# Swapping two matmuls at each seam between the w_out products and the w_in products of a second MLP layer

## Chip, core and metric

One NeuronCore of a Trainium2 chip runs the whole program. The metric is the device time in microseconds (us) from launch to end; lower is better.

## What is computed

The program is an attention (local heads and strided heads) followed by two MLP layers. Only the second layer matters here:

```
def _moe2_ref(x, w_in, w_out):
    h = np.maximum(x @ w_in, 0.0)
    return (h * h @ w_out).astype(np.float32)      # x: 2304 x 512, w_in: 512 x 2048, w_out: 2048 x 512
```

## The kernel before

Every fp32 operand is split into a high part and a remainder, so that one exact product is made of three TensorE matmuls: high by high, high by remainder, remainder by high.

Layer 2 walks over blocks of 512 tokens. After a first narrow block, four blocks `k` remain, and for each of them the 2048 columns of w_in are taken 256 at a time, `q` = 0 to 7. A step (k, q) is called a pair; there are 32 (`pairs7`). Both products of a pair are computed by a scheme with seven half-sized multiplications instead of eight. In a pair, TensorE alternates between two kinds of work, all of it in matmuls of 128 x 128 stationary by 256 moving columns:

- a **visit** (`visit`, line 1279 in the traces of this kernel) multiplies by w_in and accumulates in one PSUM bank, `ps_m`. There are four visits to a pair, of 12, 6, 12 and 12 matmuls. All four use the same bank: pool `ps_h` has a single buffer. The first matmul of each visit starts the bank afresh.
- a **gap** (`gaps`, filled by `n_unit`, line 1306) multiplies the squared activations of the pair before by w_out and accumulates in seven other banks (`ps_y`). There are four gaps, after visits 1, 2, 3 and 4, of 9, 9, 15 and 9 matmuls. I number a gap by the visit that it follows; gap 4 stands ahead of visit 1 of the next frame.

`frame` is called 31 times in `seven`, and writes one pair's order down by hand: TensorE executes the 84 matmuls of a frame in the order of the text (visit 1, gap 1, visit 2, gap 2, visit 3, gap 3, visit 4, gap 4). Between two visits, VectorE or ScalarE reads the bank of the visit that has just ended, and only after that may the next visit start it again:

- visit 1: ScalarE copies the bank out (line 1359), 128 x 512
- visit 2: VectorE adds half the bank to `c11` (helper `add`, line 1112), 128 x 256
- visit 3: VectorE reads it twice (line 1112): 128 x 512 into `u`, then 128 x 256 into `a22`
- visit 4: VectorE adds the bank to `u` and writes `c` (line 1112), 128 x 512; then it is squared (line 1288)

Each gap covers such a read. The framework puts the waits: a matmul that needs a semaphore waits with its weight load, and the instructions behind it wait with it. The w_out halves are streamed through a ring of SBUF tiles: the last matmul of a unit is followed by `ring_load` (line 1253), a DMA on SyncE's queue into the tile that this unit has just used.

Of the kernel before, what the change touches and what calls it, by code (L numbers as in the profile page):

```python
# [17 lines left out]
P = 128  # L18
# [57 lines left out]
HALF = DM // 2  # L76
# [93 lines left out]
def tile_attention_then_two_mlps(  # L170
# [9 lines left out]
    nc = tc.nc  # L180
# [258 lines left out]
    for i in range(0, half2, 2):  # L439
        n = i + 2 if i + 2 < half2 else None  # L440
# [660 lines left out]
    def high(hi, src):  # L1101
        nc.scalar.activation(out=hi, in_=src, func=AF.Copy)  # L1102
# [95 lines left out]
    def x_op(k, i):  # L1198
        at = (k - NB) % 2 * 10 + 2 * i if i < 5 else 10 + 2 * i
        return [  # L1200
            xall[:, 48 + (at + a) * TB:48 + (at + a + 1) * TB].rearrange("p (c n) -> p c n", c=2)
            for a in range(2)
        ]
# [35 lines left out]
    pairs7 = [(k, q) for k in range(NB + 1, 2 * NB) for q in range(NF // 2)]  # L1239
# [5 lines left out]
    n_use, banks, acc, of = [0], {}, {}, {}  # L1245

    def ring(u):
        return wt["in", 1, 2 * (u % (NF // 2)) + 1][:, 0]
# [18 lines left out]
    def m_weights(q, name):  # L1267
        if name[0] == "s":
            return [t[:, int(name[1]) - 1] for t in s_parts[NF + 2 * q]]
        w = wt["in", 1, 2 * q + int(name[0]) - 1]  # L1270
        return [w[:, int(name[1]) - 1, a] for a in range(2)]

    def visit(k, q, ps, *products):
        for half, (name, i) in enumerate(products):
            w_hi, w_lo = m_weights(q, name)
            x_hi, x_lo = x_op(k, i)
            for j in range(2):
                for m, (w, x) in enumerate(((w_hi, x_hi), (w_lo, x_hi), (w_hi, x_lo))):
                    nc.tensor.matmul(  # L1279
                        ps[:, half * HT:(half + 1) * HT],  # L1280
                        lhsT=w[:, j * P:(j + 1) * P],
                        rhs=x[:, j],
                        start=half == 0 and j == 0 and m == 0,
                        stop=half + 1 == len(products) and j == 1 and m == 2,
                    )
# [4 lines left out]
    def n_unit(k, q, name):  # L1290
        first, end = q == 0, q == NF // 2 - 1
        if k == last7:
            end = q == NF // 2 - 2 and name not in ("12", "s4b22")
        u = n_use[0]
        n_use[0] += 1
        w_hi, w_lo = (ring(u)[:, a] for a in range(2))

        def half(t):
            if first and t == 0:
                tag = BANK.get(name, "a")  # L1300
                pool = ps_a if tag == "a" else ps_y
                banks[name] = pool.tile([P, 512], F32, tag=tag, name="ps_y")
            h, lo = g_op(name)
            rows = slice(t * P, (t + 1) * P)
            for m, (g, w) in enumerate(((h, w_hi), (h, w_lo), (lo, w_hi))):
                nc.tensor.matmul(  # L1306
                    banks[name][:, t * HALF:(t + 1) * HALF],
                    lhsT=g[:, rows],
                    rhs=w,
                    start=first and t == 0 and m == 0,  # L1310
                    stop=end and t == 1 and m == 2,
                )
            if t:
                ring_load(u + NF // 2)

        return [lambda t=t: half(t) for t in range(2)]

    def frame(gaps, nxt, cur, copies=((), (), ()), end=False, x=((), (), ()), late=()):

        k, q = nxt  # L1320
        if not of:
            of["r"] = gpool.tile([P, TB], F32, tag="r", name="r", bufs=1)
            of["c"] = gpool.tile([P, TB], F32, tag="sq", name="c", bufs=1)
            shapes = {"bh": ("qk0", 4), "bl": ("qk1", 4), "ah": ("qk2", 3)}
            for t, (tag, n) in shapes.items():
                of[t] = fpool.tile([P, n * HALF], F32R, tag=tag, name=t, bufs=1).rearrange(
                    "p (i n) -> p i n", i=n)
            for t, n in (("al", 2), ("al2", 1)):
                of[t] = gpool.tile([P, 3 * HALF], F32R, tag="gl", name=t, bufs=2)[
                    :, 48:48 + n * HALF].rearrange("p (i n) -> p i n", i=n)  # L1330
        r, c = (of[t].rearrange("p (h n) -> p h n", h=2) for t in ("r", "c"))
        a11, a22, a21, a12 = r[:, 0], r[:, 1], c[:, 0], c[:, 1]
        ah, al, bh, bl = (of[t] for t in ("ah", "al", "bh", "bl"))
        sums_x, high_x, rest_x = x

        def positive(t, src):
            nc.scalar.activation(out=t, in_=src, func=AF.Relu)
            nc.scalar.activation(out=t, in_=t, func=AF.Square)

        if cur:  # L1340
            s13, s24 = (
                gpool.tile([P, TB + P], F32, tag="gh", name="s", bufs=2)[:, :TB].rearrange(
                    "p (i n) -> p i n", i=2)
                for _ in range(2)
            )
            high(ah[:, 2], a12)
            tt(s13[:, 0], a21, a22, ALU.add)
            tt(s13[:, 1], a11, a21, ALU.subtract)
            rest(ah[:, 2], of["al2"][:, 0], a12)
            tt(s24[:, 0], s13[:, 0], a11, ALU.subtract)  # L1350
            tt(s24[:, 1], a12, s24[:, 0], ALU.subtract)
        each(copies[0])
        ps = ps_h.tile([P, TB], F32, tag="h", name="ps_m")
        visit(k, q, ps, ("11", 0), ("s2", 1))
        m, u = (vpool.tile([P, 512], F32, tag="val", name="u") for _ in range(2))

        c11, u2 = m[:, :HT], m[:, HT:]
        u3 = u[:, HT:]
        nc.scalar.activation(out=m, in_=ps, func=AF.Copy, scale=W_BACK)
        tt(u2, c11, u2, ALU.add)  # L1360
        each(copies[1])
        if cur:
            high(ah[:, 0:2], s13)
            high(bh[:, 2:4], s24)
        each(copies[2])
        each(gaps[0])
        if end:
            first_sum()
            rest(ah[:, 0:2], al, s13)
        visit(k, q, ps, ("12", 2))  # L1370
        add(c11, ps[:, :HT], c11)
        if cur:
            rest(bh[:, 2:4], bl[:, 2:4], s24)
        if cur and not end:
            rest(ah[:, 0:2], al, s13)
        each(sums_x)
        if end:
            each(high_x)
            each(rest_x)
        positive(a11, c11)  # L1380
        high(bh[:, 0], a11)
        if not end:
            each(high_x)
        each(gaps[1])
        if nxt == pairs7[0]:
            ps = ps_a.tile([P, TB], F32, tag="a", name="ps_m")
        visit(k, q, ps, ("s1", 3), ("s3", 4))
        add(
            u.rearrange("p (h n) -> p h n", h=2),
            ps.rearrange("p (h n) -> p h n", h=2),  # L1390
            u2.unsqueeze(1).to_broadcast([P, 2, HT]),
        )
        add(a22, ps[:, :HT], u3)
        positive(a22, a22)
        high(bh[:, 1], a22)
        rest(bh[:, 0], bl[:, 0], a11)
        if not end:
            each(rest_x)
        each(gaps[2])
        each(late)  # L1400
        rest(bh[:, 1], bl[:, 1], a22)
        visit(k, q, ps, ("s4", 5), ("22", 6))
        add(of["c"], ps, u)
        squares(of["c"])
        each(gaps[3])
# [110 lines left out]
            nc.sync.dma_start(out=rows_out(1, 1)[:, a], in_=halves(o)[:, a])  # L1516

    def seven():
        copies, sums = None, []
        for n, (k, q) in enumerate(pairs7[:-1]):  # L1520
            todo = [one for name in ORDER for one in n_unit(k, q, name)]
            gaps = todo[:3], todo[3:6], todo[6:11], todo[11:]
            end = q == NF // 2 - 1 or n + 2 == len(pairs7)
            more = k < last7
            x = [[], [], []]
            if more and q == 0:
                x_work[k + 1] = x_works(k + 1)
            if more and q > 1:
                x = [list(part) for part in x_work[k + 1][q - 2]]
            late = [lambda: sums_late(not more)] if end else []  # L1530
            if sums:
                first, then = sums.pop(0)
                x[0] += first
                late += then
            frame(gaps, pairs7[n + 1], True, copies or ((), (), ()), end, x, late)
            copies = None
            if more and q in (1, 2):
                load_x(k + 1, q - 1)
            if end and more:
                copies, sums = sums_then(k)  # L1540
        finish()
# [8 lines left out]
    with tc.manual_schedule():  # L1550
# [3 lines left out]
        ps = ps_h.tile([P, TB], F32, tag="h", name="ps_w")[:, :P]  # L1554
# [19 lines left out]
        for s in range(len(steps)):  # L1574
            k, f = steps[s]
            layer, j = blocks[k]
# [81 lines left out]
```

## Time and profile before

| | |
|---|---|
| time, median of 3 runs | 860.36 us (860.15 to 861.51) |
| time of the profiled execution | 861.31 us |
| span of its profile, first to last instruction | 859.5 us |
| TensorE busy (matmul / weight load) | 847.9 us (99%) / 770.0 us (90%) |
| VectorE, ScalarE busy | 681.6 us (79%), 525.8 us (61%) |
| layer 2's pairs | from about 547 us to 849.6 us of the span |

The profile is of one execution. PE is TensorE's matmul stream, PEld its weight loads, DVE is VectorE, ACT is ScalarE, SP is SyncE. Matmuls are pipelined and overlap in the rows: the time that one costs is read from start to start, not from its own length.

### The profile page before, as it was taken

The numbers are of one execution on the slowest core, as the hardware profiler recorded it, in microseconds if no ns is written. First come the engines' busy times: TensorE is split into PE (matmuls) and PEld (weight loads), VectorE is DVE, ScalarE is ACT, GpSimd is POOL, SyncE is SP. The second block draws the span as 40 slices with busy tenths as digits, with TensorE's granted clock in tenths as the row PEclk, the third lists the DMA queues.
The fourth block names the chain that finished last, engine by engine and source line by source line (L and its number), as shares of the span: only waits on it lengthen the run. The fifth ranks groups of instructions, "written<-read, shape, count | busy, mean of one in ns | idle before, by whom it ended". The sixth has DMA issues, their size and how long they took to land. (4 is left out here: it accounts for less than half of the span.)

```text
span 859.5 us, 16041 instructions
## 1 busy us (share of the span) xinstructions
PE 847.9 (99%) x5719; PEld 770.0 (90%) x5719; DVE 681.6 (79%) x1710; ACT 525.8 (61%) x1216; POOL 17.5 (2%) x15
## 2 busy tenths in 40 slices
PE   8899999999999999999999999999999999999998
PEld 8778888888788888899888899999999999999998
DVE  5899896489775777478889996678888888888877
ACT  6987775467675666376766774455555564556442
POOL 0710000000000000000000000000000000000000
PEclk9999999999999999999999999999999999999999
DMA  8965721222222222268996476476668667766764
GB/s 257 348 216 157 239 64 45 88 78 76 73 78 98 61 71 59 74 245 295 348 364 213 157 265 239 130 225 202 188 202 281 186 194 236 238 187 198 229 188 132
DMA packets 82399, 155.21 MB, mean 181 GB/s; under 512 B 7568, under 2 KB 36368, under 8 KB 80272
## 3 DMA queue, kind: packets, MB, share of 16 engines
q1 hardware_dynamic: 82320, 154.19, 55.1%
q8 instruction: 45, 0.74, 0.3%
q14 instruction: 34, 0.28, 0.1%
HBM read 127.95 MB, written 26.21 MB: 179 GB/s over the span
## 5 line engine op out<-in xcount | busy, mean ns | idle before, releaser
L975 PE MATMUL ps_h<-xall,w 128*128 128x512 f32 (+1 forms) x1153 | 247.3, 358 | 0.0
L975 PEld LDWEIGHTS ps_h<-xall,w 128*128 128x128 f32 x1153 | 185.1, 188 | 26.0
L975 PE MATMUL ps_y<-gh,w 128*128 128x512 f32 (+1 forms) x640 | 155.7, 374 | 0.7 <-ACT gh L1024 0.7
L975 PEld LDWEIGHTS ps_y<-gh,w 128*128 128x128 f32 x640 | 107.9, 188 | 17.6 <-ACT gh L1024 1.1
L1279 PE MATMUL ps_m<-xall,s 128*128 128x256 f32 x768 | 104.5, 279 | 0.3 <-DVE r L1112 0.3
L1018 ACT ACTIVATE r<-ps_h 128x512 f32<-128x512 f32 x80 | 47.7, 597 | 86.9 <-PE ps_h L975 78.1
L1279 PEld LDWEIGHTS ps_m<-xall,s 128*128 128x128 f32 x768 | 95.5, 188 | 0.9 <-DVE r L1112 0.8
L1306 PE MATMUL ps_y<-w,bh 128*128 128x256 f32 x496 | 91.8, 278 | 0.0
L1279 PE MATMUL ps_m<-xall,w 128*128 128x256 f32 x576 | 83.4, 281 | 0.4 <-DVE c L1112 0.4
L975 PE MATMUL ps_y<-gl,w 128*128 128x512 f32 (+1 forms) x324 | 83.8, 370 | 0.0
L1306 PEld LDWEIGHTS ps_y<-w,bh 128*128 128x128 f32 x496 | 75.3, 188 | 0.0
L1279 PEld LDWEIGHTS ps_m<-xall,w 128*128 128x128 f32 x576 | 74.2, 188 | 1.1 <-DVE c L1112 0.6
L1029 DVE TENSOR_TENSOR gl<-sq,gh 128x512 fp32r<-128x512 f32 x80 | 55.3, 691 | 22.2 <-ACT gh L1024 17.5
L1306 PE MATMUL ps_y<-w,ah 128*128 128x256 f32 x372 | 70.0, 278 | 0.0
L1306 PE MATMUL ps_y<-w,bl 128*128 128x256 f32 x248 | 68.8, 277 | 0.0
L1027 DVE TENSOR_TENSOR sq<-r 128x512 f32<-128x512 f32 x38 | 26.3, 692 | 50.6 <-ACT r L1018 50.6
L975 PEld LDWEIGHTS ps_y<-gl,w 128*128 128x128 f32 x324 | 55.7, 188 | 9.6 <-DVE gl L1029 0.4
L1306 PEld LDWEIGHTS ps_y<-w,ah 128*128 128x128 f32 x372 | 56.7, 189 | 0.0
L1112 DVE SCALAR_TENSOR_TENSOR u<-ps_m,u 128x256 f32<-128x256 f32 x64 | 35.7, 557 | 25.5 <-PE ps_m L1279 25.4
L680 ACT ACTIVATE s<-s,m 96x128 f32<-96x128 f32 (+2 forms) x88 | 34.3, 390 | 34.2 <-DVE m L564 33.5
L1102 ACT ACTIVATE ah<-c 128x256 fp32r<-128x256 f32 x33 | 13.7, 418 | 63.4 <-DVE c L1288 63.4
L1306 PE MATMUL ps_y<-w,al 128*128 128x256 f32 x186 | 51.7, 278 | 0.0
(121 smaller groups left out, 1500.8 us busy)
## 6 DMA issues: line engine op xcount, KB each, us to landing
w<-w_mem SPq DMA_DIRECT2D x221, 256.0 KB, 2.8
raw<-moe_w_in_d SPq DMA_DIRECT2D x32, 512.0 KB, 5.7
raw<-moe_w_out_d SPq DMA_DIRECT2D x24, 512.0 KB, 5.2
w_mem<-xall SPq DMA_DIRECT2D x16, 512.0 KB, 3.9
w_mem<-xall SPq DMA_DIRECT2D x8, 1024.0 KB, 5.1
xall<-w_mem SPq DMA_DIRECT2D x8, 1024.0 KB, 5.4
qk<-loc_qk_d SPq DMA_DIRECT2D x12, 416.0 KB, 3.2
out_d<-o SPq DMA_DIRECT2D x17, 256.0 KB, 2.6
```

The source lines that it names most:

```text
L680: nc.scalar.activation(out=blk, in_=blk, func=AF.Exp, scale=-1.0, bias=m[:nq, j:j + 1], accum_out=dens[i][:nq, j:j + 1],)
L975: nc.tensor.matmul(y[:, c:c + w], lhsT=lhsT, rhs=rhs[:, c:c + w], start=start and c == 0, stop=stop and c + w == n,)
L1018: nc.scalar.activation(out=r, in_=ps, func=AF.Relu, scale=W_BACK)
L1027: nc.vector.tensor_tensor(out=sq, in0=r, in1=r, op=ALU.mult)
L1029: nc.vector.tensor_tensor(out=lo, in0=sq, in1=r32(h), op=ALU.subtract)
L1102: nc.scalar.activation(out=hi, in_=src, func=AF.Copy)
L1112: nc.vector.scalar_tensor_tensor(out=dst, in0=src, scalar=sign * W_BACK, in1=to, op0=ALU.mult, op1=ALU.add)
L1279: nc.tensor.matmul(ps[:, half * HT:(half + 1) * HT], lhsT=w[:, j * P:(j + 1) * P], rhs=x[:, j], start=half == 0 and j == 0 and m == 0, sto ...
L1306: nc.tensor.matmul(banks[name][:, t * HALF:(t + 1) * HALF], lhsT=g[:, rows], rhs=w, start=first and t == 0 and m == 0, stop=end and t == 1 ...
```

## The change

The last matmul of each gap and the first matmul of the visit behind it change places. For that, `n_unit` returns six single matmuls in place of two groups of three; the last one of gaps 1, 2 and 3 is taken out and handed to the next visit, which issues it behind its own first matmul; that of gap 4 is kept for visit 1 of the next frame (not for the last frame, whose gap 4 stays whole). Visits 2, 3 and 4 are called with `between[1]` to `between[3]`. The number of matmuls, their operands and their banks stay the same.

```
-    def visit(k, q, ps, *products):
+    def visit(k, q, ps, *products, between=None):
...
                 for m, (w, x) in enumerate(((w_hi, x_hi), (w_lo, x_hi), (w_hi, x_lo))):
+                    if half == 0 and j == 0 and m == 1 and between is not None:
+                        between()
                     nc.tensor.matmul(
...
-        def half(t):
-            if first and t == 0:
+        def one(t, m):
+            if first and t == 0 and m == 0:
...
-            if t:
+            if t and m == 2:
                 ring_load(u + NF // 2)
 
-        return [lambda t=t: half(t) for t in range(2)]
+        return [lambda t=t, m=m: one(t, m) for t in range(2) for m in range(3)]
...
-        visit(k, q, ps, ("11", 0), ("s2", 1))
+        visit(k, q, ps, ("11", 0), ("s2", 1), between=between[0])
...
-        copies, sums = None, []
+        copies, sums, kept = None, [], None
...
-            gaps = todo[:3], todo[3:6], todo[6:11], todo[11:]
+
+            cuts = 0, 9, 18, 33, 42
+            gaps = [todo[a:b] for a, b in zip(cuts, cuts[1:])]
+            between = [kept] + [gap.pop() for gap in gaps[:3]]
+            kept = gaps[3].pop() if n + 2 < len(pairs7) else None
...
-            frame(gaps, pairs7[n + 1], True, copies or ((), (), ()), end, x, late)
+            frame(gaps, pairs7[n + 1], True, copies or ((), (), ()), end, x, late, between)
```

## Rows read from the trace of the kernel before

**Rows 1.** The page: busy time of each engine, and the granted clock in 40 slices.
```profile
PE 847.9 (99%) x5719; PEld 770.0 (90%) x5719; DVE 681.6 (79%) x1710; ACT 525.8 (61%) x1216; POOL 17.5 (2%) x15
...
PEclk9999999999999999999999999999999999999999
```
**Rows 2.** Waits of PE from 548.6 to 849.6 us: total, times, longest.
```profile
PE ps_m L1279 <- DVE c L1112: 0.4, 1, 0.4
```
**Rows 3.** Timeline of PE, one frame: start, length of the merged rows, what.
```profile
643.61 0.40 PE L1306 MATMUL ps_y<-w,ah 128*128 128x256 f32 x2
...
644.67 0.85 PE L1279 MATMUL ps_m<-xall,w 128*128 128x256 f32 x6
645.36 0.84 PE L1279 MATMUL ps_m<-xall,s 128*128 128x256 f32 x6
646.04 0.39 PE L1306 MATMUL ps_y<-w,bh 128*128 128x256 f32 x2
...
647.06 0.87 PE L1279 MATMUL ps_m<-xall,w 128*128 128x256 f32 x6
647.77 0.40 PE L1306 MATMUL ps_y<-w,ah 128*128 128x256 f32 x2
...
648.84 1.53 PE L1279 MATMUL ps_m<-xall,s 128*128 128x256 f32 x12
650.21 0.39 PE L1306 MATMUL ps_y<-w,bh 128*128 128x256 f32 x2
...
651.91 0.87 PE L1279 MATMUL ps_m<-xall,s 128*128 128x256 f32 x6
...
653.33 0.40 PE L1306 MATMUL ps_y<-w,ah 128*128 128x256 f32 x2
...
654.39 0.85 PE L1279 MATMUL ps_m<-xall,w 128*128 128x256 f32 x6
```
**Rows 4.** Timeline of PEld, the same frame, around the first load of each visit.
```profile
644.44 0.19 PEld L1306 LDWEIGHTS ps_y<-w,bl 128*128 128x128 f32 x1
644.55 0.77 PEld L1279 LDWEIGHTS ps_m<-xall,w 128*128 128x128 f32 x6
...
646.84 0.19 PEld L1306 LDWEIGHTS ps_y<-w,al 128*128 128x128 f32 x1
646.95 0.77 PEld L1279 LDWEIGHTS ps_m<-xall,w 128*128 128x128 f32 x6
...
648.60 0.19 PEld L1306 LDWEIGHTS ps_y<-w,bl 128*128 128x128 f32 x1
...
651.68 0.19 PEld L1306 LDWEIGHTS ps_y<-w,al 128*128 128x128 f32 x1
```
**Rows 5.** Timeline of DVE, the same frame: its last read of the visits' bank.
```profile
643.81 0.69 DVE L1112 SCALAR_TENSOR_TENSOR c<-ps_m,u 128x512 f32<-128x512 f32 x1
...
647.97 0.42 DVE L1112 SCALAR_TENSOR_TENSOR u<-ps_m,u 128x256 f32<-128x256 f32 x1 [0.49 <-PE ps_m L1279]
...
651.13 0.42 DVE L1112 SCALAR_TENSOR_TENSOR r<-ps_m,u 128x256 f32<-128x256 f32 x1
```
**Rows 6.** Timeline of ACT, the same frame: the read behind visit 1.
```profile
646.24 0.60 ACT L1359 ACTIVATE u<-ps_m 128x512 f32<-128x512 f32 x1 [0.57 <-PE ps_m L1279]
```
**Rows 7.** Timeline of DVE, the frame that ends a block.
```profile
631.94 0.42 DVE L1112 SCALAR_TENSOR_TENSOR r<-ps_m,u 128x256 f32<-128x256 f32 x1
```
**Rows 8.** Timeline of PEld, the same place: last of gap 3, first of visit 4.
```profile
632.21 0.19 PEld L1306 LDWEIGHTS ps_y<-w,al 128*128 128x128 f32 x1
632.42 0.76 PEld L1279 LDWEIGHTS ps_m<-xall,s 128*128 128x128 f32 x6
```
**Rows 9.** Waits of SP's queue from 548.6 to 849.6 us: total, times, longest.
```profile
SPq L1253 <- PE ps_y L1306: 175.3, 195, 1.7
```
**Rows 10.** DMA issues: what, times, size, median us from issue to landing.
```profile
w<-w_mem SPq DMA_DIRECT2D x221, 256.0 KB, 2.8
```

More of the change, by code (lines that the diff above doesn't have):

```diff
@@ L1303, in half, with frame @@
             h, lo = g_op(name)
[L1304 to L1312, printed above, removed]
-            if t:
+            g, w = ((h, w_hi), (h, w_lo), (lo, w_hi))[m]
+            nc.tensor.matmul(
+                banks[name][:, t * HALF:(t + 1) * HALF],
+                lhsT=g[:, t * P:(t + 1) * P],
+                rhs=w,
+                start=first and t == 0 and m == 0,
+                stop=end and t == 1 and m == 2,
+            )
+            if t and m == 2:
                 ring_load(u + NF // 2)
-        return [lambda t=t: half(t) for t in range(2)]
-    def frame(gaps, nxt, cur, copies=((), (), ()), end=False, x=((), (), ()), late=()):
+        return [lambda t=t, m=m: one(t, m) for t in range(2) for m in range(3)]
+    def frame(gaps, nxt, cur, copies=((), (), ()), end=False, x=((), (), ()), late=(),
+              between=(None,) * 4):
         k, q = nxt
@@ L1369, in frame @@
             rest(ah[:, 0:2], al, s13)
-        visit(k, q, ps, ("12", 2))
+        visit(k, q, ps, ("12", 2), between=between[1])
         add(c11, ps[:, :HT], c11)
@@ L1386, in frame @@
             ps = ps_a.tile([P, TB], F32, tag="a", name="ps_m")
-        visit(k, q, ps, ("s1", 3), ("s3", 4))
+        visit(k, q, ps, ("s1", 3), ("s3", 4), between=between[2])
         add(
@@ L1401, in frame @@
         rest(bh[:, 1], bl[:, 1], a22)
-        visit(k, q, ps, ("s4", 5), ("22", 6))
+        visit(k, q, ps, ("s4", 5), ("22", 6), between=between[3])
         add(of["c"], ps, u)
```

## Prediction

> **What bounds the kernel now.** I read the page first: TensorE has work in 99% of the span, VectorE in 79%, and the granted clock never leaves its upper level, 2.4 GHz [rows 1]. Then the waits inside layer 2's pairs, where all of the change lies: one wait of 0.4 us in 301 us is all that the view shows of idle TensorE [rows 2]. So in the pairs time is made of two things: how many matmuls there are, and how far each starts behind the one before. The count does not change. What can change is the spacing, and waits too short for the wait view, which are found only by setting the timelines of the engines beside each other.
>
> The timeline of one frame gives the spacing, from start to start [rows 3]. Gap 4 takes 644.67 − 643.61 = 1.06 us for 9 matmuls, 0.118 each. Visit 1 runs 12 in 1.37, of which the last six take 0.68: 0.113 each; gap 1 runs 9 in 1.02: 0.113. Visit 2 takes 0.71 for 6 (0.118) and gap 2 1.07 for 9 (0.118). Visit 3 and gap 3 take 1.37 for 12 and 1.70 for 15 (0.114 and 0.113), visit 4 and the next gap 4 1.42 for 12 and 1.06 for 9 (0.118). One frame is 654.39 − 644.67 = 9.72 us. So there are two speeds, 0.113 and 0.118, each kind of work is met at both, and in this frame the speed changes at the first matmul of each visit and nowhere else: exactly at the seam that is edited. 36 of the 84 matmuls run at the slow speed. Made fast, they would save 36 × 0.0045 = 0.16 us a frame, 5 us in 31 frames. That is the largest gain that I see for the change.
>
> Next I set the loads beside the engines that free the bank. Each visit starts the one bank again, so its first weight load waits for the last read of it. What lies between the end of that read and the load, when nothing else is late? At the end of a block VectorE's read ends at 631.94 + 0.42 = 632.36 [rows 7], and the load starts at 632.42, although the load before it began at 632.21 and the next was due 0.113 after that, at 632.32 [rows 8]. So 0.06 us is the hand-over, and this seam waited 0.1 us without showing in the wait view.
>
> **The change part by part.** No instruction is added or removed; one matmul of a visit is issued one place (0.113 to 0.118 us) earlier, and one of a gap one place later. The moved visit matmul brings its wait along, and TensorE's stream is in order: behind it stand the gap's last matmul and then the rest of the visit. So at each seam the question is whether the bank is free 0.115 us earlier than it had to be so far. The loads of the last gap matmul mark the time at which the first one of the visit will now be due.
>
> Visit 1: VectorE's read of visit 4 ends at 643.81 + 0.69 = 644.50 [rows 5]; with the hand-over the bank is free at 644.55 to 644.56. The load ran at 644.55 [rows 4]: there is no slack at all today. In the new order it is due at 644.44. The wait is 644.55 − 644.44 = 0.115 us a frame. It cannot be moved away: the read starts 0.69 us before its end, as soon as visit 4's last matmul is done, and nothing in the edit starts it earlier. In 30 frames (the first has nothing kept): 30 × 0.115 = 3.45 us. A faster gap 4 would only lengthen the wait, so its 9 matmuls have nothing to win.
>
> Visit 2: ScalarE's copy ends at 646.24 + 0.60 = 646.84 [rows 6], bank free at 646.90. The load ran at 646.95 and will be due at 646.84 [rows 4]: a wait of 0.05 to 0.06 us. If visit 1's and gap 1's matmuls should run at the slow speed, the due time moves back by 8 × 0.0045 = 0.04 and 0.01 to 0.02 is left. I take 0.05: 31 × 0.05 = 1.55 us, with 0.4 as the other end.
>
> Visits 3 and 4: free at 647.97 + 0.42 + 0.06 = 648.45 and 651.13 + 0.42 + 0.06 = 651.61 [rows 5], due at 648.60 and 651.68 [rows 4]. They keep 0.15 and 0.07 us: no wait, the gaps' matmuls still cover the reads. In the three frames that end a block visit 4 is already late [rows 8], so the place that is lost there is lost whole: 3 × 0.115 = 0.35 us.
>
> A rule of the Trainium skill speaks on the same point, against this change: its page "PSUM — Partial Sum Buffer", section "PSUM bank collisions raise a hardware error", says that accesses of two engines are to be kept apart by bank, whatever addresses inside it they touch; so a first matmul that writes only half of the bank must still wait for the whole read. The hand-over above agrees with that: the load at 632.42 follows the end of the read. By the page alone the sum would be the same.
>
> The waits: 3.45 + 1.55 + 0.35 = 5.35 us, with a lower end of 4.2.
>
> The speeds: the trace has no place where single matmuls of the two kinds alternate, so this term must be bounded. Today there is one seam from gap to visit at each boundary, and each turns the speed over. Afterwards there are two of them at each (last but one of the gap to first of the visit; last of the gap to second of the visit). If each turns the speed over, two cancel, and the speed stays what it was; where a wait stands in place of one of them, one remains. I cannot tell which speed results. Lower end: all fast. Without gap 4, which is covered by the wait, 27 slow matmuls are left to win: 27 × 0.0045 = 0.12 us a frame, −3.8 us. Upper end: all slow; the 48 matmuls at 0.113 lose 48 × 0.0045 = 0.22 us a frame, +6.7 us, less 1.1 for the shorter wait at visit 2. Crossing itself costs: visit 1's first six take 0.69 against 0.68 for its last six [rows 3], 0.01 at a crossing. Eight more crossings a frame (two at each boundary) cost between 0 and 8 × 0.01 = 0.08 us, 0 to 2.5 us in all; I take the full price, as rows 3 show it at the nearest like crossing. For the speed itself I take half of the lower end, −1.9 us, since the waits break the stream and the seam that follows a wait today (632.42: six loads in 0.76 [rows 8], no longer than the six of 0.77 at 644.55 [rows 4]) runs fast.
>
> The DMAs: two of the four moved gap matmuls end a unit, so their ring loads are issued 0.1 to 0.3 us later, and that of gap 4 also moves past the block loads that are issued between two frames. The ring loads follow TensorE anyway, waiting for the product 195 times [rows 9], and land after 2.8 us [rows 10], while the tile is needed again more than a frame (9.72 us) later. Seven microseconds of cover hide this; without it a late load would stop TensorE for what is lacking. I price it at nothing.
>
> Sum: 5.35 + 2.5 − 1.9 = 5.95 us. The profiled execution took 861.31 us (a span of 859.5 and 1.8 around it), 0.95 above the median of the runs. On that execution the sum gives 867.3; on the median of 860.36 it gives 866.3, which is my prediction.
>
> **Rivals.** (1) All fast, crossings free: the waits of 5.35 less 3.8 leave 1.5 us, and with the lower ends of both 0.4 to 1.5: 860.8 to 861.9. For it: after the wait in rows 8 the speed is fast. Against it: each crossing seen costs something.
>
> (2) All slow: 5.35 + 6.7 − 1.1 + 2.5 = 13.4 us: 873.8. For it: every lone crossing into a visit from a fast gap ends slow. Against: two of four seams get a wait, and behind rows 8's wait the stream is fast.
>
> (3) Faster: the seam at visit 1 does not wait, because the read would be done 0.115 us sooner than I think. Place: VectorE's read behind visit 4. If it began that much earlier, the speed would decide, and 36 fast matmuls give −5 us: 855.4. It decides from a bank freed by 644.44 on. Against: the read must follow visit 4's last matmul, whose place in the stream the edit leaves alone.
>
> (4) The edit does nothing: the weight load of a waiting matmul does not hold what is behind it, and the speeds come out as now: 860.4. In the Trainium skill, "TensorE: Matmul & The Clock Gate", section "Step-by-step: what each phase is for", loads may be pulled ahead of running matmuls while matmuls keep their order; no run here shows a matmul passing a waiting one, and rows 8 show the gap's stream ending in a wait.
>
> **How the numbers follow.** Waits with speeds somewhere between the ends, 862 to 870: 0.75. Rival 1: 0.09, rival 2: 0.08, rival 3: 0.04, rival 4: 0.04. The likeliest case gives 866.3. The range 862.0 to 870.5 holds the first case and leaves out the others but for scraps. A measurement of this kernel tells about 0.2% (1.7 us) from no change. Faster is rival 3: 0.04. Same is rival 4 and most of rival 1: 0.11. Slower is the rest: 0.85.
>
> **What would show it.** In the new timeline the first load of visit 1 starts 0.06 us behind VectorE's read as now, and the gap matmul that follows it is one more behind the wait: the stretch from gap 4's first matmul to visit 1's second grows by about 0.115 us. Visit 2's first load starts 0.06 us behind ScalarE's copy. Visits 3 and 4 show no wait, except at a block's end. A frame lasts 9.72 + 0.115 + 0.05 us and what the speeds make of it. The prediction would be wrong if the seam at visit 1 shows no longer wait, or if all stretches run at one speed: then rival 1 or 2 has the time.

## The result and the profile after

The changed kernel takes 867.63 us (median of 4 runs, 866.91 to 868.06); the kernel before, run beside it, 860.78 us (4 runs, 860.15 to 861.51). The ratio is 1.0079, with an interval of 1.0061 to 1.0096, so it is slower by 5.3 to 8.3 us. The forecast was 866.3 us, in a range of 862.0 to 870.5.

The page of the profile after, busy time and granted clock, as in [rows 1]:

```profile
PE 854.6 (99%) x5719; PEld 774.9 (89%) x5719; DVE 681.6 (79%) x1710; ACT 525.8 (61%) x1216; POOL 17.6 (2%) x15
...
PEclk9999999999999999999999999999999999999999
```

The counts of instructions are those of before, and the granted clock stays at its upper level. TensorE is "busy" for 6.7 us longer with the same 5719 matmuls: a matmul that stands behind a late load is drawn longer, not as idle time. That is why the waits of PE inside the pairs again show one entry and nothing else [rows 2]; after it, the wait of SyncE's queue, and its largest issue row (issue to landing in the last column):

```profile
PE ps_m L1281 <- DVE c L1112: 0.5, 1, 0.5
```

```profile
SPq L1253 <- PE ps_y L1307: 182.2, 191, 1.7
```

```profile
w<-w_mem SPq DMA_DIRECT2D x221, 256.0 KB, 2.9
```

SyncE still waits for TensorE and not the other way round [rows 9, 10]; the moved ring loads cost nothing.

The timeline of PE shows one frame after, against [rows 3]. The first matmul of each visit now stands alone, with one of a gap behind it:

```profile
646.77 0.39 PE L1307 MATMUL ps_y<-w,bh 128*128 128x256 f32 x2
647.03 0.38 PE L1281 MATMUL ps_m<-xall,w 128*128 128x256 f32 x1
647.25 0.28 PE L1307 MATMUL ps_y<-w,bl 128*128 128x256 f32 x1
647.37 0.75 PE L1281 MATMUL ps_m<-xall,w 128*128 128x256 f32 x5
...
649.55 0.33 PE L1281 MATMUL ps_m<-xall,w 128*128 128x256 f32 x1
649.72 0.28 PE L1307 MATMUL ps_y<-w,al 128*128 128x256 f32 x1
...
651.33 0.28 PE L1281 MATMUL ps_m<-xall,s 128*128 128x256 f32 x1
651.45 0.28 PE L1307 MATMUL ps_y<-w,bl 128*128 128x256 f32 x1
...
654.51 0.28 PE L1281 MATMUL ps_m<-xall,s 128*128 128x256 f32 x1
654.63 0.28 PE L1307 MATMUL ps_y<-w,al 128*128 128x256 f32 x1
...
656.96 0.39 PE L1281 MATMUL ps_m<-xall,w 128*128 128x256 f32 x1
```

The frame is 656.96 − 647.03 = 9.93 us long, against 9.72. The lengths already tell where: the lone matmul of visits 3 and 4 is drawn 0.28 us long, that of visit 2 0.33, that of visit 1 0.38. The weight loads of the same frame, with what frees the bank (VectorE, then ScalarE), place the waits:

```profile
646.66 0.30 PEld L1307 LDWEIGHTS ps_y<-w,bh 128*128 128x128 f32 x2
647.03 0.19 PEld L1281 LDWEIGHTS ps_m<-xall,w 128*128 128x128 f32 x1
647.14 0.19 PEld L1307 LDWEIGHTS ps_y<-w,bl 128*128 128x128 f32 x1
...
649.21 0.30 PEld L1307 LDWEIGHTS ps_y<-w,ah 128*128 128x128 f32 x2
649.49 0.19 PEld L1281 LDWEIGHTS ps_m<-xall,w 128*128 128x128 f32 x1
649.60 0.19 PEld L1307 LDWEIGHTS ps_y<-w,al 128*128 128x128 f32 x1
...
651.22 0.19 PEld L1281 LDWEIGHTS ps_m<-xall,s 128*128 128x128 f32 x1
...
654.39 0.19 PEld L1281 LDWEIGHTS ps_m<-xall,s 128*128 128x128 f32 x1
```

```profile
646.28 0.69 DVE L1112 SCALAR_TENSOR_TENSOR c<-ps_m,u 128x512 f32<-128x512 f32 x1
...
650.62 0.42 DVE L1112 SCALAR_TENSOR_TENSOR u<-ps_m,u 128x256 f32<-128x256 f32 x1 [0.65 <-PE ps_m L1281]
...
653.78 0.42 DVE L1112 SCALAR_TENSOR_TENSOR r<-ps_m,u 128x256 f32<-128x256 f32 x1
```

```profile
648.84 0.60 ACT L1361 ACTIVATE u<-ps_m 128x512 f32<-128x512 f32 x1 [0.68 <-PE ps_m L1281]
```

Visit 1: the read ends at 646.28 + 0.69 = 646.97 and the load runs at 647.03. Two loads were merged at 646.66, the second of them 0.113 later, at 646.77; the next was due at 646.88. In nanoseconds the load at 647.03 lies 261 behind the one before it instead of 113: a wait of 0.148 us. The gap's product that was put behind it follows at 647.14, only after the wait. Visit 2: the copy ends at 649.44, the load runs at 649.49, 165 ns behind the one before: a wait of 0.052. Visits 3 and 4 load 651.22 − 651.04 = 0.18 and 654.39 − 654.20 = 0.19 us behind the read, and not late: no wait. So a frame has 0.148 + 0.052 = 0.200 us of waits that it did not have.

The distances of all 84 loads of one frame in nanoseconds show that this is nearly all. A `|` stands where a visit begins, with its first load right behind it; the wide space parts a visit from its gap; in the kernel after, the second number of a row is the gap's product that now stands inside the visit.

```
before |117 117 122 117 113 114 113 113 114 113 113 114  113 115 113 114 113 113 114 113 113
       |114 115 118 117 119 117  117 120 122 117 119 117 118 118 117
       |118 117 121 118 113 113 114 113 113 114 113 113  114 115 113 113 114 113 113 114 113 113 114 113 113 114 113
       |113 115 119 116 120 117 117 119 117 117 119 118  116 120 122 118 118 117 118 118 118
after  |261 108 119 117 122 120 118 113 114 113 113 114 113  113 115 114 113 113 114 113 113
       |165 109 121 117 122 120 118  113 115 114 113 113 114 113 113
       |114 115 117 116 118 117 119 118 116 119 118 117 119  117 117 122 117 118 118 117 119 117 118 118 118 117
       |118 117 120 116 123 120 117 114 113 113 114 113 113  114 115 113 113 114 113 113 113 114
```

84 products at 0.1133 us are 9.517 us. The frame before lies 0.203 us above that, the frame after 0.405 (0.409 in the median frame); less the waits of 0.200 it is 0.205 to 0.209. The longer spacing has moved (from visit 2, gap 2, visit 4 and gap 4 to visit 3 and gap 3), and what spacing and changeovers cost together is the same within 0.006 us. (Behind a seam the first five or so products lie a few nanoseconds above 113 in either kernel, with a wait ahead of them or without.)

Over all 31 frames, from the first product of visit 1 to the last product of the last gap 4, the trace after takes 308.37 us and that of before 302.27: 6.10 us more. The waits alone, 30 × 0.148 + 31 × 0.052, are 6.05 (the first visit 1 has nothing kept and so no wait). The profiled executions differ by 868.06 − 861.31 = 6.75; 0.63 of it lies ahead of the pairs, where the two kernels are alike: the first visit 1 is loaded at 547.14 us of the span before and at 547.77 after. In the traces of the experiments whose kernels are alike up to there it comes between 546.72 and 547.54 us, so single executions differ by that much without the edit.

### The profile page after: what moved, and what is told of

The parts are those of the page before. It is cut to its first block, busy times and chain, and to the rows that moved or that the text cites. A ratio compares the mean times of both kernels' runs of the same rounds, so it can differ in the third digit from the quotient of the medians.

```text
span 866.3 us, 16043 instructions
## 1 busy us (share of the span) xinstructions
PE 854.6 (99%) x5719; PEld 774.9 (89%) x5719; DVE 681.6 (79%) x1710; ACT 525.8 (61%) x1216; POOL 17.6 (2%) x15
## 5 line engine op out<-in xcount | busy, mean ns | idle before, releaser
L1281 PE MATMUL ps_m<-xall,s 128*128 128x256 f32 x768 | 112.9, 280 | 0.3 <-DVE r L1112 0.3
L1281 PEld LDWEIGHTS ps_m<-xall,s 128*128 128x128 f32 x768 | 101.1, 189 | 0.9 <-DVE r L1112 0.8
L1281 PE MATMUL ps_m<-xall,w 128*128 128x256 f32 x576 | 94.3, 287 | 0.5 <-DVE c L1112 0.5
L1281 PEld LDWEIGHTS ps_m<-xall,w 128*128 128x128 f32 x576 | 78.3, 188 | 3.3 <-DVE c L1112 0.7
```

The costliest lines, as they stand in the source:

```text
L1281: nc.tensor.matmul(ps[:, half * HT:(half + 1) * HT], lhsT=w[:, j * P:(j + 1) * P], rhs=x[:, j], start=half == 0 and j == 0 and m == 0, sto ...
```

## The experiments

Each ran five rounds beside the kernel before. "Frame" is the median distance from one visit 1's first matmul to the next one's. Theory W holds that the waits of the first products make the time; theory C, that what it costs to pass between the two kinds of product does. Diffs are against the changed kernel, unless the text says otherwise.

**Only visit 1's seam swapped.**

```
-            between = [kept] + [gap.pop() for gap in gaps[:3]]
+            between = [kept, None, None, None]
```

> The swap at visit 1's seam alone (gaps 1 to 3 keep their order). Theory W (the time is the waits for the bank: in the changed kernel's trace 0.148 us at visit 1 and 0.052 at visit 2 of a frame that grew from 9.720 to 9.925 us): gap 4 should run at the slower spacing as before, so visit 1 waits 0.115 us, frame 9.83 to 9.85 us, 3.4 to 4 us over before, about 864.3. Rival C (each swapped seam costs the same, 0.205 / 4 = 0.05 us, for crossing between the two kinds of products): frame 9.77, 1.6 us over before, about 862.3.

864.02 us against 860.91, ratio 1.004 (1.0028 to 1.0053); frame 9.833 us, 0.113 more than before. Its weight loads and VectorE's read at visit 1:

```profile
664.91 0.19 PEld L1307 LDWEIGHTS ps_y<-w,bh 128*128 128x128 f32 x1
665.14 0.19 PEld L1281 LDWEIGHTS ps_m<-xall,w 128*128 128x128 f32 x1
```

```profile
664.39 0.69 DVE L1112 SCALAR_TENSOR_TENSOR c<-ps_m,u 128x512 f32<-128x512 f32 x1 [0.15 <-PE ps_m L1281]
```

The load follows the read's end (665.08) by 0.06 us and the load ahead of it by 0.23 instead of 0.118: a wait of 0.115, precisely what the prediction worked out, because here gap 4 still has the longer spacing. One seam makes 3.1 of the 6.85 us. W holds; C, which had a frame of 9.77, does not.

**Only the seams of visits 3 and 4 swapped.**

```
-            between = [kept] + [gap.pop() for gap in gaps[:3]]
+            between = [None, None] + [gap.pop() for gap in gaps[1:3]]
```

(`kept` is removed with it.)

> The swap at the seams of visits 3 and 4 alone, where VectorE has freed the bank 0.15 and 0.07 us before the earlier load. Theory W: no wait but 0.115 us in the three frames that end a block; a frame of 9.72 to 9.76 us, 0 to 1.5 us over before, 860.8 to 862.3. Rival C (every swapped seam costs 0.05 us): frame 9.82, 3.2 us over before, about 864.

861.70 us against 860.91, 1.0008 (0.9999 to 1.0017); frame 9.733, 0.013 above before. The first loads of visits 3 and 4 are not late:

```profile
668.64 0.19 PEld L1307 LDWEIGHTS ps_y<-w,bl 128*128 128x128 f32 x1
...
668.99 0.19 PEld L1281 LDWEIGHTS ps_m<-xall,s 128*128 128x128 f32 x1
669.11 0.19 PEld L1307 LDWEIGHTS ps_y<-w,bl 128*128 128x128 f32 x1
...
672.09 0.19 PEld L1281 LDWEIGHTS ps_m<-xall,s 128*128 128x128 f32 x1
672.20 0.19 PEld L1307 LDWEIGHTS ps_y<-w,al 128*128 128x128 f32 x1
```

Two seams, each with two more changes between the kinds of product, cost 0.013 us a frame together, where the prediction had 0.01 for each change. Without a wait the edit can't be told from no change. And each of them turns the spacing once, as the plain seam does, though it passes from w_out to w_in twice.

**A longer gap 4.** The gap ahead of visit 1 gets one product more, gap 3 one less, the swaps stay.

```
-            cuts = 0, 9, 18, 33, 42
+            cuts = 0, 9, 18, 32, 42
```

> All four swaps, and one product of gap 3 moved into gap 4 (14 and 10 in place of 15 and 9), so that VectorE's read behind visit 4 is covered by as many products as before the change. Theory W: visit 1's wait falls from 0.148 to 0.035 us, visit 4 still finds its bank free (it kept 0.13), frame 9.81 us, 3.4 us under the changed kernel, about 864.2. Rival C: the crossings are the same, frame 9.92, no change against the changed kernel, about 867.6.

863.29 us, 1.003 (1.0019 to 1.0042), 0.005 below the changed kernel's ratio; frame 9.780, in most frames 9.780 to 9.794. VectorE's read and the first load of visit 1:

```profile
654.22 0.69 DVE L1112 SCALAR_TENSOR_TENSOR c<-ps_m,u 128x512 f32<-128x512 f32 x1
```

```profile
654.96 0.19 PEld L1281 LDWEIGHTS ps_m<-xall,w 128*128 128x128 f32 x1
```

The load still follows the end of the read (654.91) by 0.05 us, but its distance from the load ahead of it falls from 261 to 149 ns, a wait of 0.036 in place of 0.148: one product's 0.113 us of cover takes 0.112 us of wait away. W had 9.81 by counting this alone. The frame is shorter still by 0.02 to 0.03. Visit 3's and gap 3's longer spacing covers one product less, which is 0.005; the rest lies in the first products behind the seams of visits 1, 2 and 4, which come 0.014, 0.008 and 0.009 us sooner than in the changed kernel. Why they do is not shown.

**Visit 4's bank read in half the time.** The read of `c` takes only the half of the bank; the other half of `c` is left without the product's part.

```
-        add(of["c"], ps, u)
+        add(of["c"][:, :HT], ps[:, :HT], u[:, :HT])
+        tt(of["c"][:, HT:], u[:, HT:], u[:, HT:], ALU.add)
```

> All four swaps, but behind visit 4 VectorE reads only half of the bank (128 x 256, some 0.42 us in place of 0.69); the other half of c is filled from u, so part of the product of x and w_in is left out. The bank is free 0.27 us earlier, everything else is as in the changed kernel. Theory W: visit 1's wait of 0.148 is gone; frame 9.78 us if visit 1 and gap 1 keep the shorter spacing, up to 9.86 if the seam without a wait turns it over; 2 to 4.6 us under the changed kernel. Rival C: 9.92, no change.

863.41 us, 1.0029 (1.0019 to 1.0038); frame 9.800. VectorE's read and the loads at visit 1:

```profile
665.27 0.42 DVE L1112 SCALAR_TENSOR_TENSOR c<-ps_m,u 128x256 f32<-128x256 f32 x1 [0.20 <-PE ps_m L1281]
665.61 0.42 DVE L390 TENSOR_TENSOR c<-u 128x256 f32<-128x256 f32 x1
```

```profile
665.64 0.30 PEld L1307 LDWEIGHTS ps_y<-w,bh 128*128 128x128 f32 x2
665.86 0.19 PEld L1281 LDWEIGHTS ps_m<-xall,w 128*128 128x128 f32 x1
665.98 0.19 PEld L1307 LDWEIGHTS ps_y<-w,bl 128*128 128x128 f32 x1
```

The read ends at 665.69, 0.17 us ahead of the load, and the load comes 0.113 behind the one before: the wait is gone, and it was the read that made it. But the frame falls by 0.125 and not by 0.148. With the wait gone, this seam too turns the spacing: visit 1 and gap 1 now run at 0.118, together some 0.06 us dearer, of which the shorter wait at visit 2 (0.024 in place of 0.052) gives a part back. In these frames the spacing is 0.113 behind a seam with a wait, and a seam without one turns it.

**The gap's product one place or two deeper in the visit.** If a seam turns the spacing and a second seam turns it back, the longer one might be cut out. At visits 3 and 4 the gap's last product is put behind the third product of the visit, or behind the second; visits 1 and 2 stay plain, gaps of 8, 9, 16 and 9 products.

```
-                    if half == 0 and j == 0 and m == 1 and between is not None:
+                    if half == 0 and 3 * j + m == 3 and between is not None:
...
-            cuts = 0, 9, 18, 33, 42
+            cuts = 0, 8, 17, 33, 42
...
-            between = [kept] + [gap.pop() for gap in gaps[:3]]
+            between = [None, None] + [gap.pop() for gap in gaps[1:3]]
```

(With `== 2` in the second kernel. Here and in the next kernel `kept` is removed too.)

> Gaps of 8, 9, 16 and 9 products; the last one of gaps 2 and 3 (those in front of visits 3 and 4) comes back behind the third product of the visit, all else in plain order. Visits 3 and 4 then have 8 and 15 products ahead of them and their banks are free 0.1 and 0.19 us early; visit 2 waits 0.05, visit 1 0.03. Theory T (every step from a w_out product to a w_in product that does not wait turns the spacing over, when the one before has had time to settle): at visits 3 and 4 the spacing turns to 0.118 and back within four products, the rest of the frame runs at 0.113: frame about 9.68 us, 1 us under before. Rival S (a seam turns the spacing once, however its products are mixed, as the seams of the changed kernel did): visit 3 and gap 3 run at 0.118, frame 9.75 us, 1 us over before.

> The same with the gap's product behind the second product of visits 3 and 4. Theory T, if two products are enough to settle: frame about 9.67 us, 1 to 1.5 us under before. Rival S: as in the run with three, 9.75 us, 1 us over before.

Behind the third: 864.96 us against 860.66, 1.0049 (1.0036 to 1.0061), frames from 9.71 to 9.92, median 9.76. Behind the second: 862.59, 1.0022 (1.0012 to 1.0031), frame 9.734. Visit 3 of the second, loads, with the nanoseconds of the same stretch under it:

```profile
668.09 0.19 PEld L1307 LDWEIGHTS ps_y<-w,bh 128*128 128x128 f32 x1
668.20 0.30 PEld L1281 LDWEIGHTS ps_m<-xall,s 128*128 128x128 f32 x2
668.44 0.19 PEld L1307 LDWEIGHTS ps_y<-w,bh 128*128 128x128 f32 x1
668.55 1.24 PEld L1281 LDWEIGHTS ps_m<-xall,s 128*128 128x128 f32 x10
669.72 0.19 PEld L1307 LDWEIGHTS ps_y<-w,bl 128*128 128x128 f32 x1
```

```
|113 115 [118] 117 122 117 119 115 123 119 113 114 113  113 115 114 113 113 ...     [118] is the gap's product
```

The spacing does turn, and turns back: the rest of the visit and all of gap 3 run at 0.113. That half of the idea was right. But the products between the two turns lie 2 + 5 + 4 + 9 + 4 + 6 + 2 + 10 + 6 = 48 ns above 113, 0.05 us a seam, so the two seams take back 0.1 us a frame. And where gap 4 runs at 0.113 its nine products are done 0.04 us sooner while the read is not: visit 1 waits 0.035. Of the 36 products at the longer spacing before, the nine of gap 4 can't be won. The first of the two has a profiled execution of 862.26 us while its other four runs took 864.9 to 865.7, so its profile does not account for its time. It does hold frames of two kinds. Visit 2 and gap 2, in one frame of each kind:

```
|165 109 121 115 123 119  113 115 114 113 113 114 113 113
|167 108 118 117 119 118  116 120 122 117 119 117 118 118
```

Visit 2 waits 0.05 us in both, but behind the wait the spacing is 0.113 in 22 of the 31 frames and 0.118 in nine, where a frame lasts some 0.12 us longer (9.875 and 9.753 in these two). If the longer one stood in all frames of the other executions, they would take some 22 × 0.12 = 2.6 us more, 864.9: an estimate, and not shown, as no other execution was profiled. So a wait does not always bring the shorter spacing. Both kernels are over the kernel before, by 4.3 and 1.9 us, where theory T had them 1 to 1.5 under.

**Other lengths of the gaps, nothing swapped.** Gap 1 gets 11 products and gap 3 13.

```
-            cuts = 0, 9, 18, 33, 42
+            cuts = 0, 11, 20, 33, 42
...
-            between = [kept] + [gap.pop() for gap in gaps[:3]]
+            between = [None] * 4
```

> The order of before with other gap lengths: 11, 9, 13 and 9 in place of 9, 9, 15 and 9, no product exchanged. Visit 4 then waits 0.04 us and visit 1 0.03; a seam with a wait has kept the shorter spacing in every trace so far, so only visit 2 and gap 2 run at 0.118 (15 products in place of 36). Frame 9.70 us against 9.72; the three block ends lose 0.2 us each: 0 to 0.5 us under before, too little to be told. Rival (a wait does not keep the spacing): 9.79 us, 2 us over before.

862.58 us, 1.0023 (1.0014 to 1.0032). The frames are uneven, 9.68 to 9.96, median 9.729. With two products less ahead of it, visit 4's first load is late in most frames (distance 153 ns, a wait of 0.04), and behind that wait the spacing was 0.113. Near the three block ends the missing cover was paid for with waits of 0.10 us at visit 4 and 0.19 at visit 1, and behind those the spacing was 0.118. So the run is 1.9 us over before, and not under it as expected. Nor had a wait kept the shorter spacing "in every trace so far": at one of the three block ends of the kernel before, visit 4 waits 0.09 us and 0.118 follows.

Then two orders against the kernel before, with `n_unit` changed to single matmuls as in the change: gaps of 9, 7, 17, 9 and of 9, 8, 16, 9 products. The first of them:

```
-            gaps = todo[:3], todo[3:6], todo[6:11], todo[11:]
+            gaps = todo[:9], todo[9:16], todo[16:33], todo[33:]
```

> The order of before, no product exchanged, with gaps of 9, 7, 17 and 9 products: visit 3's read-out has 0.15 us and more to spare, so two products of gap 2 (at 0.118) go to gap 3 (at 0.113), and visit 4 no longer waits 0.09 us where a block ends. From the rows: frame 9.71 us in place of 9.72, block ends 0.09 shorter: 0.3 + 0.3 us, 0.5 us under before at the most, which is less than a measurement can tell. If gap 2 of seven products is too short for VectorE's read, visit 3 waits and the frame grows by some 0.05 us, 1.5 us over before.

1001.33 us, 1.1638 (1.16 to 1.1675), a frame of 14.17 us: far off. One product with the second part of `bh` now stands behind the place where ScalarE rewrites `bh` for the next pair (the other that was moved reads `bl`, which is rewritten later); it reads that pair's factor, and TensorE waits for it every time. The waits of PE inside the pairs, and one place in PE's timeline with ScalarE's write:

```profile
PE ps_y L1305 <- ACT bh L1102: 81.6, 31, 3.1
```

```profile
648.01 1.57 PE L1279 MATMUL ps_m<-xall,s 128*128 128x256 f32 x12
...
652.17 0.39 PE L1305 MATMUL ps_y<-w,bh 128*128 128x256 f32 x1 [2.58 <-ACT bh L1102]
```

```profile
651.70 0.42 ACT L1102 ACTIVATE bh<-r 128x256 fp32r<-128x256 f32 x1
```

81.6 us in 31 times is 2.6 us a frame, of 14.17 − 9.72 = 4.45. The page of the profile shows where another part comes from, in the granted clock of its 40 slices:

```profile
PEclk9999999999999999999999998889888798888878
```

With TensorE pausing in each frame the mean of the clock falls to 0.941; slices of 8 are a mean of its two levels, so parts of them ran at 1.2 GHz. How the rest divides was not worked out. The bank `ps_m` has no share in this: the expectation failed on a product that the new lengths had moved behind the next writer of its factor.

In the second the middle slices are `todo[9:17]` and `todo[17:33]`.

> Mends the run before, where gap 2 of seven products left two products with bh's second part behind the instruction that fills it for the next pair: TensorE waited for ScalarE 2.6 us a frame, and those two products took the factor of the wrong pair. With gaps of 9, 8, 16 and 9 only the product with bl is left behind, which is filled later. Theory: no wait for ScalarE; one product of 36 moves from 0.118 to 0.113 and visit 4's 0.09 us at three block ends go: 0.1 + 0.3 us under before, 860.3, which no measurement here can tell. Rival: the wait comes from the gap's length alone, then visit 3 waits for VectorE and the frame is over 9.72 us.

The expectation speaks of two products that took the wrong factor; by the rows above it is one. The run takes 860.86 us against 861.05, 0.9997 (0.9988 to 1.0007); frame 9.720, nothing changed. No order that was tried beats the kernel before.

**The remainders moved in SBUF.** Against the kernel before: the tiles of the remainders of the squared activations (`al` in the rows, and its second) begin 48 columns, 192 bytes, earlier. Same instructions, same order.

```
-                    :, 48:48 + n * HALF].rearrange("p (i n) -> p i n", i=n)
+                    :, :n * HALF].rearrange("p (i n) -> p i n", i=n)
```

> The order of before; only the remainders al and al2 of the w_out products are placed 48 columns (192 bytes) lower in their tiles. This asks whether the turns of the spacing come from where the operands lie. If the SBUF addresses of the stationary and the moving operand decide, the spacing changes at the remainder products of gaps 1 to 4 (6 in a frame use al or al2) and the frame's length with it, by up to 0.2 us either way (6 us in all). If the kind of work or the waits decide, the trace is that of before, 9.72 us a frame.

864.31 us, 1.0046 (1.0034 to 1.0059); frame 9.867. The weight loads of gap 3, the first of each triple:

```profile
670.89 0.31 PEld L1306 LDWEIGHTS ps_y<-w,bh 128*128 128x128 f32 x2
...
671.25 0.31 PEld L1306 LDWEIGHTS ps_y<-w,bh 128*128 128x128 f32 x2
...
671.60 0.30 PEld L1306 LDWEIGHTS ps_y<-w,ah 128*128 128x128 f32 x2
...
671.96 0.31 PEld L1306 LDWEIGHTS ps_y<-w,ah 128*128 128x128 f32 x2
```

A triple takes 0.36 us or 0.35, so 0.118 a product, in a gap that ran at 0.113 before [rows 3]. In other gaps of this kernel the spacing changes inside the gap, at a product with a remainder (114 115 113 115 120 117 117 ns at the start of gap 4). Where an operand lies in SBUF is thus part of what sets the spacing, with no wait and no other order of work.

## Why the prediction was right, and where not

**The hand-over and the wait at visit 1: right.** The load comes 0.05 to 0.06 us behind the read in both traces; the wait is the read's, as its shortening showed. Its size was 0.115 in the kernel with this seam alone, and 0.148 in the changed kernel, since gap 4 there runs at 0.113 and comes to the same read 9 × 0.0045 = 0.04 us sooner. The prediction had named that ("would only lengthen the wait") but left the term at 0.115: 30 × 0.148 = 4.4 us, not 3.45.

**Visit 2: right.** 0.052 measured, 0.05 taken: 31 × 0.052 = 1.6 us.

**Visits 3 and 4: right**, no wait; both swaps alone gave 0.8 us with an interval that takes in no change. At the block's ends the term was too large: the three frames are 10.01, 10.02 and 10.01 us, against 9.76, 9.81 and 9.77 before, so they lost 0.26, 0.21 and 0.24, of which 0.206 is any frame's; 0.09 us in all, not 0.35. The weight loads there, at visit 4:

```profile
634.22 0.30 PEld L1307 LDWEIGHTS ps_y<-w,ah 128*128 128x128 f32 x2
634.55 0.19 PEld L1281 LDWEIGHTS ps_m<-xall,s 128*128 128x128 f32 x1
```

The second load of the first row is 0.113 us in, at 634.33, and visit 4's comes 0.22 behind it: a wait of 0.1 us. The plain seam already waited about as long [rows 8], with one product more ahead of it. The spacing makes up for the product: visit 3 and gap 3 run at 0.118 in the changed kernel, and the 26 steps from visit 3's first load to the last load ahead of visit 4 take 3.06 us there, 2.96 before. So 0.10 us of the 0.115 is covered again.

**The step that failed is the speeds.** The prediction held that if each change of product turned the spacing over, the two turns at a swapped seam would cancel, left open which spacing results, and took +2.5 us for the crossings and −1.9 for the speed. The runs show that in both kernels a seam without a wait turns the spacing once, plain or swapped. In the changed kernel all 59 such seams did, and behind all 64 seams with a wait the spacing was 0.113; so the longer spacing stayed, but moved to other visits. By the list of distances crossings and speed together are some 0.005 us a frame, 0.2 us, in place of +0.6. Split at 0.0045 us a product, 27 products at the longer spacing in place of 36 save some 1.3 us over 31 frames, and the first products behind the seams cost some 1.4 more: an estimate, with the signs that the prediction had given the two terms.

That the total came so near is partly luck. The wait at visit 1 was put 1 us too low, the speeds and crossings 0.4 too high and the block ends 0.3 too high, and these errors nearly cancel: 5.95 us forecast, 6.10 measured over the 31 frames.

**The DMAs: right**, no wait for a ring tile appears. **The rivals:** neither all at the shorter spacing nor all at the longer. That a waiting load lets others by is refuted by the load at 647.14: of loads pulled ahead, of which the Trainium skill's page "TensorE: Matmul & The Clock Gate" speaks under "Step-by-step: what each phase is for", the runs show none that passes a waiting load. Whether a first product that writes the half of a bank that is already read could start sooner was not tried.

**Left open:** what makes a seam turn the spacing. It goes with a wait at the seam, with the depth at which the gap's product stands and with the operands' places in SBUF. The wait alone does not decide it: counted over the traces of ten kernels (without the two of 9, 7, 17, 9 products and of the moved remainders, and without the seams whose product stands deeper), 705 of 714 seams without a wait turned the spacing; behind 386 with a wait it was 0.113 at 359 and 0.118 at 27. The timed runs of the kernel with the product behind the third stay open too.

## What to carry to other kernels

When TensorE is never idle by the wait view, measure the distance from load to load at each place where a bank changes hands: waits of 0.05 to 0.15 us are there, drawn as busy, and thirty frames make microseconds of them. Work that covers a read must stand ahead of the first instruction that needs the bank, all of it; one product moved behind that instruction cost its full length where the cover had no slack, and nothing that could be measured where it had. And what a stretch gains in spacing is worth nothing if a read, not the stretch, sets when the next one may begin.

## What the hardware showed that I had not expected

- Two steady spacings of the same 128 x 128 by 256 matmul at the same granted clock, 0.113 and 0.118 us, that persist over up to 27 products in the changed kernel, and over three visits and their gaps with the remainders moved. They change where the kind of product does, or at a product with a remainder once that lies elsewhere. 192 bytes in the place of a remainder made the kernel 0.46% slower (9.720 to 9.867 us a frame).
- Behind a wait at a seam the spacing was the shorter one at 359 of 386 seams. In the kernel with half the read that was worth some 0.06 us: taking a wait of 0.148 us away gained 0.125.
